# Turning attention tiles on TensorE instead of by transposing transfers, in a fused attention and ELU layer kernel

## The chip, the cores and the metric

The kernel runs on one core of one Trainium2 chip. A core has five engines with a queue each: TensorE (PE, with PEld for its weight loads), VectorE (DVE), ScalarE (ACT), GpSimd (POOL) and SyncE (SP), and 16 DMA engines. The metric is the time on the device in microseconds.

## The reference, cut to what matters

```python
# q, k, v: [8, 8, 576, 64] (batch, head, position, depth)
scores = scale * np.matmul(q, k.transpose(0, 1, 3, 2))
bias = slopes[:, None, None] * (-np.abs(rel).astype(np.float32))[None, :, :]
mask = (rel >= 0) & (rel < window)                      # window = 128
scores = np.where(mask, scores + bias[None], -1000000000.0)
scores = scores - np.max(scores, axis=-1, keepdims=True)
attn = np.exp(scores)
attn = attn / (np.sum(attn, axis=-1, keepdims=True) + 1e-09)
attn_out = np.matmul(attn, v)
x = attn_out.transpose(0, 2, 1, 3).reshape(B * S, H * D)        # [4608, 512]
h = x @ w_in                                                    # [4608, 2048]
g = np.where(h > 0.0, h, alpha * (np.exp(np.minimum(h, 0.0)) - 1.0))
out = g @ w_out                                                 # [4608, 512]
```

A causal attention with a sliding window of 128 positions and a linear bias by distance, and behind it two dense layers with an ELU between them.

## The kernel before

**Attention.** Each batch of 576 positions is cut into key blocks of 128 (`u`). `scores` (L215) computes four groups of heads at once, each on 32 rows of the array, into four PSUM banks `sp[0]` to `sp[3]`. The first two banks are one tile, `spa`, the other two are the tiles `sp2` and `sp3`. `expo` (L227) takes the exponential on ScalarE: one instruction over both banks of `spa` (L230), and one each for `sp2` and `sp3` (L233). `weigh` (L236) multiplies by the table of the bias and the mask on VectorE. `all_values` (L263, matmuls at L271) multiplies by V for 128 query positions at a time, with a column of ones in V that gives the sum; `rden` is its reciprocal (L277), and L279 writes the normalised tile `xn` (positions by 512 features). The fifth tile of a batch has 64 positions and goes through `values` (L240) in two parts. The first two batches have loads and scores of their own (`turn_first`, `first_scores` and so on).

**Turning.** The dense layer needs the features on the partitions, so each `xn` is turned into a ring `xT` that holds three batches. Nine tiles, those of batch 0 and the first four of batch 1, are turned by TensorE: `turn_x` (L289) issues four transposes against the identity (L295) into a PSUM bank, and ScalarE or VectorE copies the result to `xT` (L297). The other 31 tiles go through `turn` (L283): one transposing transfer on SP's queue (L287), from `xn` to `xT`.

**Dense layers.** `hidden` (L304) computes a piece of x @ w_in in a PSUM bank, mostly `hp[0]` and `hp[1]` in turn, eight matmuls of 256 columns at L312. ScalarE makes the exponential of the negative part of it: a relu and an exponential (L319, L321) where the step is in the set `SOFT`, or one exponential (L323) with a clamp on GpSimd (L325). `elu` (L329) forms g on VectorE (L333). The second layer, from block 1 on, works on blocks of 256 tokens, 18 in all, each by seven products of half size (`product`, L397, matmuls at L403) instead of eight, with sums on VectorE (`sums`, `combine`, `lower`, through `add`, L364), copies on ScalarE (`keep`, L410 and L412) and stores on SP's queue (`put`, L434). Its banks are `op` and `av`, for block 1 also `sp[3]`.

**What sets the order.** All work of the main part is called by a long string of letters, `SCRIPT` (L539): each letter takes the next call from its own list, and so fixes the order in every engine's queue. `h` is the matmuls of `hidden`, `p` and `q` its two steps behind them, `e` the elu, `o` one matmul of a product (`o5` five of them), `k` the scores, `x`, `y`, `z` the exponentials, `w` the weighting, `v`, `r`, `n` the values, their reciprocal and their normalising, `T` a transposing transfer, `t` the transposes of `turn_x` and `tA` or `tD` its copy, `d` VectorE's turning of q and k, `s1` to `s4`, `c1` to `c4`, `u` and `m` the rest of a product block, `l` a load, `P`, `U` and `Z` the last block. An engine works its queue in order and waits at an instruction whose inputs or whose bank are not free.

Of the kernel before, what the change touches and what calls it, by code (L numbers as in the profile page):

```python
# [7 lines left out]
F32 = mybir.dt.float32  # L8
F16 = mybir.dt.float16
# [9 lines left out]
def kernel(  # L19
# [57 lines left out]
    sp = [spa[:, 0, :], spa[:, 1, :]] + [ps_s.tile([128, 512], F32, name=f"sp{i}", tag=f"sp{i}") for i in (2, 3)]  # L77
# [72 lines left out]
    with tc.manual_schedule():  # L150
# [76 lines left out]
        def expo(b, u, g):  # L227
            if g < 2:
                if g == 0:
                    nc.scalar.activation(unit(b, u)[:, 0:2, :, :], spa.rearrange("p g (h c) -> p g h c", h=2),  # L230
                                         AF.Exp, scale=0.125)
                return
            nc.scalar.activation(unit(b, u)[:, g, :, :], sp[g].rearrange("p (h c) -> p h c", h=2),  # L233
                                 AF.Exp, scale=0.125)
# [48 lines left out]
        def turn(b, i):  # L283
            n = 128 if i < 4 else 64
            o = (b * S + 128 * i) % RING
            x = xnt.pop((b, i)).rearrange("p g h d -> p (g h d)")
            nc.sync.dma_start_transpose(out=xT[:, :, o:o + n], in_=x[0:n, :])  # L287

        def turn_x(b, i, copy, bank):  # L289
            n = 128 if i < 4 else 64  # L290
            o = (b * S + 128 * i) % RING
            x = xnt.pop((b, i)).rearrange("p g h d -> p (g h d)")
            t = bank.bitcast(F16)[:, 0:512].rearrange("p (c r) -> p c r", c=4)
            for c in range(4):
                nc.tensor.transpose(t[:, c, 0:n], x[0:n, 128 * c:128 * c + 128], ident[0:n, 0:n])  # L295
            yield
            copy(xT[:, :, o:o + n], t[:, :, 0:n])  # L297
# [222 lines left out]
        for b in range(2, B):  # L520
# [19 lines left out]
            f fD f fD b f fA f fD C C C C b i j i j j b i j j v r n v r n b t tD v r n v r n  # L540
            h p q t tD f fA
            e h p q i j f fD f fA f fD b b i j i l
            h p q e j j l
            h p q e b i l
            h p q j v r n v r n e l
            h p q t tD b i j e l
            h p q e
            h p q e
            h p q e v r n v r n
            h p q e l O  # L550
            h p q e v r n t tA l
            h p q e a v r n l l l O
            h p q e a t tA
            h p q e a l O
            h p q e a l O O1 O2
            h p q e a l O
            h p q e a f fD f fA l l O
            h p q e a f fA f fD f fA f fA l l O
            e a l l s1 s3 O O1 O2 i j i j j
            W l l o7  # L560
            s2 W l l o1 u o6 v r n i j i j j
            l l o2 c1 o5 v r n
            W W d l o3 u o4 t tA i j v r n
            W l s4 o4 u o3 v r n
            h p q v r n i j d l
            h p q e W t tA d l o5 u o2
            h p q e v r n i j l
            h p q e W t tA l o7 c2
            h p q e v r n i j d l
            h p q e W l o7 u  # L570
            h p q e v r n v r n l c3 m s1
            o1 h o2 p o1 k l q o1 e o1 v y l t tA d o1
            h x r n e o1 T o1 p o4 s2 u
            h q w o2 e o2 z o4 d p o1
            h w q c1 o2 p v e o4 q o1 r
            h s3 u n o2 p o2 e o1 T o1 u k s4 q o1
            h x e d o2 p o3
            h w u q y l o1 z e o4 p o2 d o1
            h d q w l o1 e v p o2 c2 l o1 q o1
            h r n l o1 e o1 T p o2 l o2 s1 o1 q k l u o1 e o1 x  # L580
            h l d o2 p o1 s2 o4 u
            h w q y e o4 z o2 c3 o2 p o2 w m
            h q c1 v u e p o4 s3 o1 q o1
            h r n o2 p o1 e o1 T o1 k q s4 u
            h e x d o3 p o2 w o1
            h y q z l o1 e o1 u o3 p o1 w o2
            h q d l o1 v c2 p e o1 l o2 q o2 r o2 v l u e v o2
            h r l s1 n o2 p o2
            h r T n q n o2 p e k u d o1 q o3
            h x s2 e o2 p o3 w o3 q o1  # L590
            h c1 y e o1 z o2 s3 o2 p o3 w o1
            h u q c3 v m e T o3 u o2 r o1 p s4 o3
            h n q o1 e T o1 p k d u q
            h x l e o2 p o1 w o4 z o1 q
            h c2 y l e o2 p o2 w l o4 q
            h s1 l e o1 v l p o2 r o1 q l
            h n u d o2 p k e q o3 s2 o2 u
            h x e s3 o2 p o3
            h w q c1 y o1 e o4 z o2 c3 o2 p o1 s4
            h m T u w q o4 e v u p o2 r o3 n o1 q o1  # L600
            h T e o3 u k p c3 q
            h x l e o2 p o2 w o3 y o1 q
            h c2 z l e o2 p o2 w l o2
            h q s1 l v e p l o2 r o1 u v d q o1 m l o1
            h e o1 n o1 p o4 v r T q s2 o3
            h u e o1 s3 o1 p o2
            h r n q c1 o2 n p o3 e o1 T o2 q k d u
            h x e s4 o2 p o1
            h w z d q o5 u o2 e o1 p o4 y o2 q o1
            h u w o1 e o1 p o3 v c3  # L610
            h q r n l o2 e p o1 T o2 l o2 s3 q k l u c2
            h x e m l o3 p
            h w l q s1 l o2 z o2 e o3 y o5 p o1 w
            h q s2 v u e p o4 c1 o1 q
            h r n o2 e p o1 T o4 u s4 k q
            h x e d o2 p o3
            h w u q o1 y o1 e o4 p o2 d o1
            h z q u w l o2 p o3 e o2 v q
            h l r e o1 l n o1 p o5 s3 l T q k c2 u l e
            h x l o2 p o1 w o1  # L620
            h l q s1 o1 z o1 e o4 y o2 c3 o2 p
            h w m q s2 o1 v u p o1 v r o1 e o2 q o1 v c1 o3 e o1
            h u n o2 r p o1 T o1 n
            h r q n o2 T p e o3 k u s4 q
            h x e o2 d o1 p o4
            h z w q y e o2 u o2 p o2 w o4 q
            h c2 l e o2 p v l o2 r o2 s1 q o1
            h l u n o1 l o1 e p o1 T o2 k d l q o1
            h x e o2 p o1 w
            h u s2 q o3 z o1 e o4 y o2 c3 o1  # L630
            h p w m q c1 o1 v e o4 u o2 r o1 p
            h n q s3 T k p e o2 q o1 d o3
            h x e o1 s4 u o3 p
            h w z q o3 l u o1 e o2 p o4 y o1 c2 o1 q o1
            h w l v e p l o2 r o2 c3 o1 l o1 u
            h n q l s1 T m o2 p k e l q s3 o1
            h l x e l o1 s2 o1 p o5 d u o2 q o1
            h z e o1 y o2 w o2 p o2
            h w q c1 o2 e p v v q r o2 s4 o1
            h u e o2 n p v o3 r o1 q T o1 n o3 r o1 u o1 n o1  # L640
            h u e T d o1 k p o1 q x
            h e o2 p o1 w o4 y
            h q c2 z l e o2 p o3 w l o3 q
            h s1 l e o2 p v l o2 r o1 u
            h s2 q l n o2 p o2 c3 o3 u e o1 m T q k d
            h x e o2 p o1 w o1
            h q c1 o1 z o1 e o4 y o2 s3 o2 p
            h w q o2 v u e p o3 s4 o1 u o2
            h q r n o2 p o1 e o1 T o1 k q d
            h x e o2 u o1 w o1 p o5 y o1 q o3 z  # L650
            h e c3 o2 p
            h c2 w q o3 p v e u o2 r o1 q o1 m o1 n
            h s1 T o1 k p e u d q o3
            h x s2 e o2 p o4 c1 o1 z o2 s3 o1
            h q y e o3 p o2 w o2 u o2
            h q w e o2 p v s4 o1 u o1 v q r o2 r v
            h e n o2 p o2 r o1 T n o1
            h n q T e k p o1 u o1 q o1 x o3
            h c2 e o2 s3 p o4
            h y s1 q w o2 p o3 e o2 z o2 c3  # L660
            h u w q m o1 e v p o4 s2 u o2 q
            h r n o2 p o1 e o1 T o2 k q c1
            h x e o2 p o1 w o1
            h u q o2 z o1 e o4 p o2 s4 o2 y o1
            h q w o1 u o1 v e p o2 r o1 q u
            h n e T o2 p o2 k q o1 x o2
            h c2 e y o3 s1 p
            h q s2 o4 e o2 u o3 z o1 w o2
            h p w q o4 u o1 e v p o2 r o1 q o1
            h n s4 o1 k p e q c1 o3 c3  # L670
            h x e m T o1 s3 o1 p o3
            h w u q o1 z o1 e o4 y o4 p o1
            h w q o1 v u e p v o3 q o1 u o1
            h e o1 r o1 p o1 r o1 n o1
            h q c2 T v e p o6 s1 q o2
            h u r e o2 n p o3 c3 o1
            h q s2 e o2 p o4 n o1 u o1
            h s3 q T m e o2 p o3 c1 o2
            h q e o2 p o5
            h q u e o2 p o3 s4 o2  # L680
            h q u e o2 p o5
# [166 lines left out]
```

## Time and profile before

| | |
|---|---|
| time, median of 3 runs | 304.71 us (304.34 to 305.03) |
| the profiled execution: its time, its span | 304.94 us, 303.2 us |
| TensorE, weight loads | 296.2 us (98%), 255.6 us (84%) |
| VectorE, ScalarE, GpSimd | 256.2, 238.2, 109.1 us |
| transposing transfers `xT<-xn` | 31, median 3.1 us from issue to landing |
| nine tiles turned by TensorE | 36 matmuls at L295; copies on ScalarE 0.58 us (64 rows: 0.35) |

The span runs from the first to the last instruction of the profiled execution. "Busy" is the time in which an engine has an instruction under way. Matmuls overlap in the array, so a matmul's own duration is longer than its share of TensorE's time: that is read from the distance between starts. A chain is followed back from the last instruction, at each step to what released it.

### The profile page before, as it was taken

The page shows a single profiled execution, that of the slowest core. Times are in us where ns is not written, and L with a number is a line of the kernel's source. Part 1 is how long each engine was busy: PE and PEld are TensorE (multiplying, and loading weights), DVE is VectorE, ACT ScalarE, POOL GpSimd, SP SyncE. Part 2 cuts the span into 40 slices and gives each one's busy share as a digit, 9 for nine tenths or more (in the row PEclk, how much of TensorE's full clock was granted, in tenths as well). Part 3 has the DMA queues.
Part 4 walks back from the last instruction along what each step waited for, and adds up shares of the span by engine and source line. Part 5 has one row for each costly group of instructions (what it writes and reads, how often), then busy time and mean ns, then how long its engine had stood idle before and what let it go on. Part 6 is the DMA issues. An engine that isn't in the chain of part 4 may idle for free.

```text
span 303.2 us, 9837 instructions
## 1 busy us (share of the span) xinstructions
PE 296.2 (98%) x4074; PEld 255.6 (84%) x4074; DVE 256.2 (85%) x499; ACT 238.2 (79%) x445; POOL 109.1 (36%) x163
## 2 busy tenths in 40 slices
PE   7899999999999999999999999999999999999996
PEld 5688876989888889988888888887899888898885
DVE  5747879989999999799989898989989887885873
ACT  5577688869797888877979888888887888868881
POOL 8947958671534243332534162606000100010000
PEclk9999999999999999999999999999999999999999
DMA  8999999999394949491969695999220301111013
GB/s 99 193 198 201 201 178 192 125 128 101 36 160 72 131 78 119 83 184 21 161 60 130 107 118 66 130 144 125 61 89 2 97 17 54 54 56 43 37 57 118
DMA packets 96941, 32.04 MB, mean 106 GB/s; under 512 B 83968, under 2 KB 92800, under 8 KB 96896
## 3 DMA queue, kind: packets, MB, share of 16 engines
q0 software_dynamic: 75920, 18.36, 66.6%
q1 hardware_dynamic: 20832, 12.98, 18.0%
q8 instruction: 32, 0.52, 0.7%
q14 instruction: 13, 0.11, 0.1%
q10 hardware_dynamic: 144, 0.07, 0.1%
HBM read 36.70 MB, written 9.44 MB: 152 GB/s over the span
## 4 chain that ended last, share of the span: by engine, by line
PE 86%; DVE 4%; DMA 4%; ACT 2%; POOL 2%; issue 1%; POOLq 0%; DVEq 0%; ACTq 0%
PE hp L312 38%; PE op L403 15%; PE av L403 14%; PE spa L222 4%; PE spa L271 3%; DMA VP<-in_v_dram 2%; PE sp L403 2%; PE sp L312 2%; DMA xT<-xn 2%; PE sp L250 1%; DVE g L333 1%; PE op L339 1%; PE spa L339 1%; ACT e L323 1%; DVE xn L259 1%
## 5 line engine op out<-in xcount | busy, mean ns | idle before, releaser
L312 PE MATMUL hp<-xT,wi 128*128 128x256 f16 (+3 forms) x1488 | 144.1, 245 | 0.9 <-DMA xT<-xn 0.4
L312 PEld LDWEIGHTS <-wi 128*128 128x128 f16 x1600 | 120.6, 98 | 15.1 <-issue 3.9
L333 DVE SCALAR_TENSOR_TENSOR g<-e,hp 128x512 f16<-128x512 f32 x138 | 93.9, 681 | 23.4 <-ACT e L321 12.0
L325 POOL TENSOR_SCALAR e<-e 128x512 f32<-128x512 f32 x44 | 28.9, 657 | 151.4 <-ACT e L323 148.6
L319 ACT ACTIVATE e<-hp 128x512 f32<-128x512 f32 x98 | 58.7, 599 | 28.2 <-PE hp L312 22.9
L321 ACT ACTIVATE e<-e 128x512 f32<-128x512 f32 x100 | 63.6, 636 | 2.2
L403 PEld LDWEIGHTS <-S 128*128 128x128 f16 x544 | 51.0, 98 | 6.6 <-issue 1.1
L403 PEld LDWEIGHTS <-g 128*128 128x128 f16 x400 | 37.1, 98 | 5.4 <-issue 1.5
L238 DVE TENSOR_TENSOR EX<-EX,TAB 128x1024 f16<-128x1024 f16 x48 | 33.0, 694 | 2.8 <-ACT EX L233 1.3
L114 POOL DMA_DIRECT2D VP<-in_v_dram x40 | 34.4, 874 | 1.7 <-DMA s<-in_k_dram 1.3
L323 ACT ACTIVATE e<-hp 128x512 f32<-128x512 f32 x40 | 24.2, 605 | 12.1 <-PE hp L312 12.0
L403 PE MATMUL op<-T,S 128*128 128x256 f16 x192 | 29.5, 273 | 0.0
L403 PE MATMUL av<-T,S 128*128 128x256 f16 x176 | 27.0, 273 | 0.0
L233 ACT ACTIVATE EX<-sp 128x512 f16<-128x512 f32 x48 | 27.0, 602 | 0.0
L230 ACT ACTIVATE EX<-spa 128x1024 f16<-128x1024 f32 x24 | 24.5, 1022 | 1.0 <-PE spa L222 0.5
L364 DVE TENSOR_TENSOR S<-g 128x1024 f16<-128x1024 f16 (+2 forms) x35 | 23.1, 666 | 0.3 <-PE op L403 0.2
L403 PE MATMUL op<-wo,g 128*128 128x256 f16 x128 | 20.4, 273 | 0.0
L403 PE MATMUL av<-wo,g 128*128 128x256 f16 x120 | 19.7, 273 | 0.0
L108 POOL DMA_DIRECT2D st<-in_k_dram x24 | 16.3, 687 | 2.9 <-DMA s<-in_q_dram 2.0
L279 DVE TENSOR_TENSOR xn<-spa,rden 128x512 f16<-128x512 f32 x24 | 16.5, 687 | 0.4
L108 POOL DMA_DIRECT2D st<-in_q_dram x24 | 15.9, 666 | 1.3 <-DMA VP<-in_v_dram 1.3
L222 PE MATMUL spa<-QT,KT 32*128 32x256 f16 (+2 forms) x240 | 15.1, 250 | 0.0
(137 smaller groups left out, 381.5 us busy)
## 6 DMA issues: line engine op xcount, KB each, us to landing
out_dram<-ob SPq DMA_DIRECT2D x32, 256.0 KB, 3.2
VP<-in_v_dram POOLq DMA_DIRECT2D x32, 128.0 KB, 6.1
st<-in_k_dram POOLq DMA_DIRECT2D x24, 144.0 KB, 5.3
st<-in_q_dram POOLq DMA_DIRECT2D x24, 144.0 KB, 5.9
wi<-in_moe_w_in_dram POOLq DMA_DIRECT2D x4, 512.0 KB, 11.2
wo<-in_moe_w_out_dram POOLq DMA_DIRECT2D x4, 512.0 KB, 10.8
out_dram<-ob SPq DMA_DIRECT2D x7, 128.0 KB, 1.7
VP<-in_v_dram POOLq DMA_DIRECT2D x8, 64.0 KB, 6.1
```

Of the source, the lines that this page charges most:

```text
L108: nc.gpsimd.dma_start(st[b][32 * g:32 * g + 32, w, :, :, :, :].rearrange("p h n j d -> p (h n) (j d)"), (q, k)[w][b, 2 * g:2 * g + 2, :, : ...
L114: nc.gpsimd.dma_start(VP[b % 2][0:p, n, :, 0:D], v[b, :, 128 * n:128 * n + p, :].rearrange("h p d -> p h d"))
L222: nc.tensor.matmul(sp[g][:, 256 * h2 + o:256 * h2 + o + n], kt_[b % 2][r, k0:k0 + 255:2], qt_[b % 2][r, c0:c0 + 2 * n - 1:2], start=dh == ...
L233: nc.scalar.activation(unit(b, u)[:, g, :, :], sp[g].rearrange("p (h c) -> p h c", h=2), AF.Exp, scale=0.125)
L238: V.tensor_tensor(out=e, in0=e, in1=TAB[:, int(u == 3), 2 * gp:2 * gp + 2, :, :], op=ALU.mult)
L312: nc.tensor.matmul(p[:, l * w + u0:l * w + u1], w_in_sb[:, c, fc * 128:(fc + 1) * 128], xT[:, c, x0:x0 + u1 - u0], start=(c == 0), stop=(c ...
L319: nc.scalar.activation(e[:, 0:n], p[:, 0:n], AF.Relu, scale=-1.0)
L321: nc.scalar.activation(e[:, 0:n], e[:, 0:n], AF.Exp, scale=-1.0)
L323: nc.scalar.activation(e[:, 0:n], p[:, 0:n], AF.Exp)
L325: nc.gpsimd.tensor_scalar(out=e[:, 0:n], in0=e[:, 0:n], scalar1=1.0, scalar2=0.0, op0=ALU.min, op1=ALU.max)
L333: V.scalar_tensor_tensor(out=gs[t][:, f0:f0 + nf, c0:c0 + w], in0=sh(es.pop((t, c0, f0))), scalar=1.0, in1=sh(hps.pop((t, c0, f0))), op0=A ...
L403: nc.tensor.matmul(o, a[:, j, :], b[:, j, :], start=j == 0 and i in (1, 2, 5), stop=j == 7, skip_group_check=True)
```

## The change

`sp2` and `sp3` become one tile of two banks, `spb`, as `spa` is already, and `expo` takes one exponential over both banks of it. `turn` and its transfers are gone: all 31 tiles go through `turn_x` with the bank `sp[3]`, which is the second half of `spb`, and with ScalarE's copy. The letters `z` and `T` go, 31 times `t` and `tA` come, and the script is written anew around them.

```diff
     spa = ps_s.tile([128, 2, 512], F32, name="spa", tag="spa")
-    sp = [spa[:, 0, :], spa[:, 1, :]] + [ps_s.tile([128, 512], F32, name=f"sp{i}", tag=f"sp{i}") for i in (2, 3)]
+    spb = ps_s.tile([128, 2, 512], F32, name="spb", tag="spb")
+    sp = [t[:, i, :] for t in (spa, spb) for i in range(2)]
...
         def expo(b, u, g):
-            if g < 2:
-                if g == 0:
-                    nc.scalar.activation(unit(b, u)[:, 0:2, :, :], spa.rearrange("p g (h c) -> p g h c", h=2),
-                                         AF.Exp, scale=0.125)
-                return
-            nc.scalar.activation(unit(b, u)[:, g, :, :], sp[g].rearrange("p (h c) -> p h c", h=2),
+            nc.scalar.activation(unit(b, u)[:, g:g + 2, :, :], (spa, spb)[g // 2].rearrange("p g (h c) -> p g h c", h=2),
                                  AF.Exp, scale=0.125)
...
-        def turn(b, i):
-            n = 128 if i < 4 else 64
-            o = (b * S + 128 * i) % RING
-            x = xnt.pop((b, i)).rearrange("p g h d -> p (g h d)")
-            nc.sync.dma_start_transpose(out=xT[:, :, o:o + n], in_=x[0:n, :])
-
-        def turn_x(b, i, copy, bank):
+        def turn_x(b, i, copy, bank, c0=0):
...
-            t = bank.bitcast(F16)[:, 0:512].rearrange("p (c r) -> p c r", c=4)
+            t = bank.bitcast(F16)[:, c0:c0 + 512].rearrange("p (c r) -> p c r", c=4)
...
         for b, i in [(1, 4)] + [(b, i) for b in range(2, B) for i in range(5)]:
-            job("T", turn, b, i)
+            parts(turn_x(b, i, copies[0], sp[3]), "t", "tA")
...
-                for g, x in ((0, "x"), (2, "y"), (3, "z")):
+                for g, x in ((0, "x"), (2, "y")):
```

Of the script, one batch's stretch, before and after:

```diff
-            h q s2 v u e p o4 c1 o1 q
-            h r n o2 e p o1 T o4 u s4 k q
-            h x e d o2 p o3
-            h w u q o1 y o1 e o4 p o2 d o1
-            h z q u w l o2 p o3 e o2 v q
+            h c1 q s4 o2 y o1 e o6 c3 o2 p
+            h w m q w t u o2 e o1 tA v p o2 r o1
+            h n q d u o2 t o1 e o1 tA o5 p o1 k u q c3
+            h x l e s3 o2 p
+            h w y q o3 l o1 e o2 p o4 w l o1
```

The end of the script changes too: one of the last block's products (`P`) and several single ones (`o`) now stand before or between the last steps of `hidden` and `elu`.

More of the change, by code (lines that the diff above doesn't have):

```diff
@@ L539 @@
         SCRIPT = """
[L540 to L576, printed above, removed]
-            h x e d o2 p o3
-            h w u q y l o1 z e o4 p o2 d o1
-            h d q w l o1 e v p o2 c2 l o1 q o1
-            h r n l o1 e o1 T p o2 l o2 s1 o1 q k l u o1 e o1 x
@@ L581 @@
[L581 to L613, printed above, removed]
-            h q s2 v u e p o4 c1 o1 q
-            h r n o2 e p o1 T o4 u s4 k q
-            h x e d o2 p o3
-            h w u q o1 y o1 e o4 p o2 d o1
@@ L618 @@
-            h z q u w l o2 p o3 e o2 v q
[L619 to L681, printed above, removed]
-            h q u e o2 p o5
-            h q e o2 p o3 c2 o2
-            h s1 q u e o2 p o3 s3 o2
-            h q e o2 p o3 s2 o2
-            h q u e o2 p o3 s4 o2
-            h q c1 e o2 p o3 c3 o2
-            h q m u e o2 p o5 q u
-            h p q e s3 o5 u o2
-            h p q e s1 s2 o7 c2
-            e s1 s2 P U o7 u
-            c4 P c1 s4 P U P U
-            P U P c4 c2 Z
+            f f fD b fD f f fA b fD i C C C i j b C i j v v b r j n r j n t j tD v v r
@@ new lines @@
+            h n r n p t f tD q fA
+            h e f i fD f j f fA fD b p b i q i j
+            h l e
+            h p q b p
+            h l e j j q v i p r l n v
+            h j r q n e t l p b e i q tD
+            h j l v p
+            h r e q v p
+            h e q n
+            h r p e q v n p O e q
+            h r a l e
+            h p a q t O n tA l e p v
+            h l q l O e p r l n q
+            h a l e t p
+            h a l q
+            h p e l O a l p tA O l q q l e
+            h a l f e p l f s3 q l
@@ new lines @@
+            h fA e l O fD p l O q l s1 O1 f s2 l O2 f fA e f l f fD O fA fA l i O1 a o3 l j o1 a O2 o2 i l o1 j o1 W i j o5 u o1 W o1 j v o1 i r c1 o2 j o1 n o1 v o1 j i r n o3 W o2 u t o1 W o1 tA o1 v o2 j d o3 r
+            h s4 W v p i n
+            h u r q j n d l o2 e o2 p o1 v W o2 q t
+            h r tA l n e o2 p i d v u q
+            h j r n l e o1 t p o2 d o1
+            h tA q W l e o1 i p v d j
+            h q c2 r l e o2 p o2 n o2
+            h W q l e v p o1 v r o1
+            h r q u n s1 l o2 p t n o1 l o1 e o1 tA v o1 q k r l n s2 o1 x o3
@@ new lines @@
+            h e y s3 o2
+            h w p w u o3 q o5 p o1 e o1 t o1 q
+            h tA e v c1 p o1
+            h r u n q o1 d o2 p o1 t e o2 tA o3 c3 o2 q o1 s4 m k e
+            h x o1 u o2 w o1 p
+            h d u q y o2 d o1 l o2 e o2 p o4 w o2 q
+            h c2 l e o1 v p d l
+            h r q n l o2 c3 p o1 t l s1 o2 tA o4 e l q k u
+            h e l x m s2 o2 p o2 w
+            h u s3 q o2 p o1 e o4 y o2 c1 o2
+            h q w o2 p o1 v e u o2 q r o1
+            h n d t o2 tA o1 e o3 p k d q o1 s4 o1
@@ new lines @@
+            h x e o2 d p
+            h u q w y o3 l o1 e o3 p o2 w o1
+            h u q d l v p c2 v r l o2 e q o5 l o1 e
+            h l r n v p o1
+            h r n u n q o1 s1 o2 p o1 t e o2 tA o4 c3 u k q s2 m o1
+            h x e s4 o2 p o3 w o3 q o2 c1 o1
+            h y e o1 s3 o2 p o2
+            h w u q o2 p e t v o1 q o1 r o1
+            h n u tA e o2 p t o1 d o2 tA o1 q o3 u o1 k l e
+            h x o2 p o1 w o3
+            h y q c2 l e o2 p o4 w o2 l q o2
+            h s1 u l e v p l o2 r o1
@@ new lines @@
+            h q n l s2 o2 p k e q o5 x
+            h e s3 u o2 p o1
+            h c1 q s4 o2 y o1 e o6 c3 o2 p
[3 more added lines that the diff above has]
+            h w y q o3 l o1 e o2 p o4 w l o1
+            h q c2 l e v p l o1 s1 o1 v q
+            h l s2 u m o1 e o1 p o4 r o2 n u o1
+            h q r e v p o3 r o2 n
+            h q n d t o2 c1 tA o3 e o2 p t o1 d o1 tA o1 u k q d
+            h x e o2 s4 p o3
@@ new lines @@
+            h w q y o1 e o8 p
+            h w u q o1 v p o1 e o3 u o1 q o1 r o1
+            h n l c2 o2 c3 p t l o1 e o2 tA o3 q k l u
+            h e x m l o2 p
+            h w l q s1 l o3 p o1 e o4 y o2 s2 o4
+            h q w u v e p o2 r o1
+            h q n c1 o2 e p t o3 tA o1 s3 o3 u k s4 q
+            h x d e o2 p o3 d o2 u o1
+            h q w y o1 e o6 p o1 w o3 u o1 v q o1 l
+            h e r c2
+            h p n q o1 t p o2 l o1 e o1 tA o3 k c3 u l q s3 m l
+            h x e l o2 p o1 w
@@ new lines @@
+            h l q s1 l o2 y o1 e o8 p
+            h w q s2 o1 v u e p v o2 r o1 q o1 c1 o1 v r
+            h r e o1 n o1 p o4
+            h n q n u e o1 t o2 tA o1 d o4 p t
+            h tA q o1 u o1 e p k s4 o1 q x
+            h e o1 y o2 w o6 p o1
+            h c2 u q w o2 p l v e o4 q r
+            h l n s1 o2 l p t o1 e o2 tA o1 k l s2 q d u
+            h x l e o2 p o1 w o1
+            h u s3 q o2 p o1 e o4 y o3 c1
+            h q w o3 p o1 v e o2 r o2 c3 u
+            h q n m o1 e o1 p t o2 d o1 tA o4 q k u e
@@ new lines @@
+            h x d
+            h p s4 y q o1 w o4 l o2 e o1 u o2 p o5 c2 o1 q o1
+            h w l e o1 v p l
+            h r q l n o1 s1 l p t o2 tA o1 e o1 l o1 k q s2 l e o1 x
+            h l o1 u o1 w o1 p o4 s3 o1 u o2 q o4 c1 o1 y o1
+            h e s4 o2 p o3 w
+            h q c3 u v m e p v r o2 q r o2 n o1 v o2 r
+            h n n e o2 p o2 t o1 u o2 tA
+            h q t e o2 tA o1 p k d u q
+            h x e o2 p o4
+            h y q c2 c3 l o1 e o1 p o4 w o2 l q o2
+            h w u l m e v p o3 r o1 s1 l o2 q o2
@@ new lines @@
+            h n u l e o2 p o1 t d o1
+            h tA s2 q k p e o1 x o2 s4 o3
+            h c1 q w y o3 e o5 p
+            h w q s3 o3 u v e p o2 r o2 q
+            h n u e t o2 d tA o5 p k u q
+            h x e o2 p o1 w o4 y o1 q o1
+            h e o2 p o1 c2 o2
+            h w q u o1 e o1 p v o2 q r
+            h n s3 o1 t o2 tA s1 o4 p k e u s2 q o3
+            h x e d o2 p o4 c1 o2 q
+            h w y e o4 s4 o2 p
+            h w q o1 c3 o1 p o1 v e m u v q r o1 v r o1 n o1 u
+            h r n n o2 p o2 e o2 t q o2 tA o1
@@ new lines @@
+            h e t o2 tA o1 p k u q
+            h x e o2 p o2 c2 o3 s1 o1 q o1
+            h y e o3 w o2 p
+            h w q o3 u o1 e v p o3 r o1
+            h q n u s2 t p o3 e o2 tA o3 s3 o1 q k e
+            h x c1 o2 p o1 w o4 u o1 s4
+            h q y e o7 p o1 w
+            h q c3 v m u e p o4 r o1 u
+            h q n e t o2 tA o5 p k c2 q
+            h x e o2 p o2 s1 o4 q o1 w o3
+            h u e y s2 o3
+            h p w q o4 u o1 e o1 p o2 v q
+            h r n o2 e p o2 k c3 q c1 m o1 x
@@ new lines @@
+            h e o1 y
+            h w s4 p o4 s3 o1 u t q o2 w o3 p o3 e o2 u o2 q v
+            h tA r e o1 v p v o2 u o1 q o1
+            h e o2 p r o2 n
+            h q r c2 o2 e p o6 n q o2
+            h n e o2 s3 p o2
+            h u s1 q o2 p o1 e o3 t q o1 s2 o2
+            h u e tA o1 s4 o1 p o2 t c1 o2 tA
+            h q e o2 p o4 c3 o1
+            h q m u e o2 p o4
+            h q u e o2 p o6 q s3
+            h u e o2 p o4
+            h q e o2 p o4 c2 o2 q
+            h s1 u e o2 p o2 s2 o2
@@ L694 @@
+            h q e o2 p o6 q
+            h u e o2 p o2 s4 o3
+            h q c1 e o2 p o5
+            h q u e o2 p o3 c3 o2
+            h q m u e o2 p o5 s3 o1 q
+            h u e o2 p o3 s1 o1 P q c2 s2 o2 U o1 e o4 P u s1 s2 c4 P c1 s4 P U P U P U c4 c2 Z
         """
```

## The prediction

> **What bounds the kernel now.** I read the page's first two parts, then the chain that ended last, then the waits of TensorE alone, then busy time by stretch, and last the timeline of TensorE around the places that the change touches.
>
> ```profile
> PE 296.2 (98%) x4074; PEld 255.6 (84%) x4074; DVE 256.2 (85%) x499; ACT 238.2 (79%) x445; POOL 109.1 (36%) x163
> ...
> PE   7899999999999999999999999999999999999996
> ...
> PEclk9999999999999999999999999999999999999999
> ```
>
> TensorE is busy in nearly every slice, at the full granted clock; VectorE and ScalarE are not full. A busy PE need not be a fast one, so the pace has to be read too. Start times in the timeline of TensorE (columns: start, duration, what, count) give it:
>
> ```profile
> 102.66 1.04 PE L312 MATMUL hp<-xT,wi 128*128 128x256 f16 x8
> 103.53 0.49 PE L403 MATMUL av<-wo,g 128*128 128x256 f16 x3
> 103.86 0.82 PE L403 MATMUL op<-T,S 128*128 128x256 f16 x6
> 104.51 1.04 PE L312 MATMUL hp<-xT,wi 128*128 128x256 f16 x8
> ```
>
> Eight matmuls of 256 columns start 0.87 us before what follows, so 0.109 us each; nine of L403 take 103.53 to 104.51, again 0.109 each. The groups follow each other with no hole. This is the stream itself, not a queue waiting inside a busy bar. The chain that ended last, by engine, says the same:
>
> ```profile
> PE 86%; DVE 4%; DMA 4%; ACT 2%; POOL 2%; issue 1%; POOLq 0%; DVEq 0%; ACTq 0%
> ```
>
> Of the waits of TensorE, longest in total first (columns: us, times, longest), one concerns the transposing transfers:
>
> ```profile
> PE hp L312 <- DMA xT<-xn: 0.4, 1, 0.4
> ```
>
> And busy time in one long stretch (its length, then PE, PEld, DVE, ACT, POOL):
>
> ```profile
> 60.00:293.00 233.00, 232.38 (x3032) 203.50 (x3030) 205.30 (x385) 192.77 (x366) 65.15 (x93) 1.00 0.71 89
> ```
>
> TensorE lacks only 233.00 - 232.38 = 0.62 us here, and 0.4 us of that is the only wait for a transposing transfer in the whole run. All 31 of these transfers lie in this stretch (issued from 70.0 to 272.2 us), and so will what replaces them. The chain's 2% for "DMA xT<-xn" is one 4.68 us transfer at 200.4 us; the chain walks through its whole duration, but TensorE worked beside it and lost only that wait.
>
> **The change, part by part.**
>
> *The transposes on TensorE.* 31 tiles x 4 = 124 matmuls are added; nothing else on TensorE changes in number. The kernel already turns nine tiles this way (L295), so their price is in the trace:
>
> ```profile
> 60.44 0.39 PE L295 MATMUL av<-ident,xn 128*128 128x128 f16 x4
> 60.66 0.49 PE L403 MATMUL op<-wo,S 128*128 128x256 f16 x3
> ...
> 34.13 0.67 PE L312 MATMUL hp<-xT,wi 128*128 128x128 f16 x9
> 34.73 0.29 PE L295 MATMUL sp<-ident,xn 64*128 64x64 f16 x4
> 34.95 0.56 PE L312 MATMUL sp<-xT,wi 128*128 128x128 f16 x7
> ```
>
> A full tile's four take 60.66 - 60.44 = 0.22 us. A tile of 64 rows (the fifth of a batch) takes 34.95 - 34.73 = 0.22 us, and the nine matmuls before it take 0.60 us where nine of 128 columns at 0.056 are 0.50, so 0.10 us goes to the change of tile shape: 0.32 us in all. Six batches with four full tiles are 24 x 0.22 = 5.3 us, seven short tiles (batch 1's and those of the six) are 7 x 0.32 = 2.2 us. Sum **7.5 us**, on the engine that has 0.62 us of holes there. It goes on the path in full.
>
> Here a rule of the Trainium skill is to be weighed. "VectorE: DVE Perf Modes", section "The three transpose paths", gives 390 ns for a 128x128 transpose on TensorE against 1309 ns on the DMA crossbar, and its rules for kernel authors advise TensorE wherever a PSUM destination is acceptable. Read as speed, it promises a gain: this trace too has a transfer landing 3.1 us after issue at the median, against about a microsecond for four transposes and a copy. But it compares latencies, and a tile's latency cost this kernel 0.4 us once. What counts is the time that TensorE is occupied. Its 390 ns taken as occupancy would be an estimate of 124 x 0.39 = 48 us (353 us in all); the row's 0.22 us for four, in a stream, makes it 7.5. I take the row.
>
> *The transfers that go.* SP's queue loses 31 issues of about 1.2 us each (median 1196 ns), which stood between the stores of the output. Nothing on the path waits for those stores, so I put the relief at nothing; it would count only if the output buffers came free late, and no engine is seen waiting for them. POOL's queue of loads keeps its transfers. Their landing may come sooner; no wait for them stands in 60 to 293 us on TensorE. What is surely saved is the wait at 205.24 us, whose matmul starts 0.67 us after one that needs 0.11: **-0.56 us**.
>
> *The copies and the exponentials on ScalarE.*
>
> ```profile
> L233 ACT ACTIVATE EX<-sp 128x512 f16<-128x512 f32 x48 | 27.0, 602 | 0.0
> L230 ACT ACTIVATE EX<-spa 128x1024 f16<-128x1024 f32 x24 | 24.5, 1022 | 1.0 <-PE spa L222 0.5 <-PE sp L222 0.4
> L297 ACT COPY xT<-av 128x512 f16<-128x512 f16 x3 | 1.7, 582 | 0.1
> L297 ACT COPY xT<-sp 128x256 f16<-128x256 f16 x1 | 0.4, 353 | 0.0
> ```
>
> Added: 24 x 0.58 + 7 x 0.35 = 16.4 us. Saved: 24 units, each 2 x 0.602 - 1.022 = 0.18, so 4.4 us. ScalarE goes from 238 to about 250 us, and in the stretch from 192.8 of 233 to 204.8 of about 240, 83% to 85%. It doesn't become the bound. Its own saving is worth nothing on the path.
>
> *New waits.* Three are added to TensorE's queue, and everything behind the waiting instruction (the next 8 of L312 and the products of L403) waits with it, and then L319/L323 and L333 behind that. (a) The transposes wait for xn: after the last matmul of the weighted values VectorE needs 0.20 (L277) + 0.69 (L279), and the last matmul's own 0.19. The new order usually leaves one L312 group and five products between, 0.87 + 5 x 0.109 = 1.42 us, against 1.08 plus whatever VectorE has in front; one more L333 at 0.68 is already too much. (b) The next scores write the bank that the copy has to empty: often two products (0.22) before the copy's place and three to five (0.33 to 0.55) after it, about 0.55 to 0.77 us against 0.58 plus ScalarE's backlog. (c) L312 reads xT after the copy; one to two microseconds are left, ample. Also the copy pushes the chain L319, L321, L333, which frees hp for the L312 after next, by 0.58, while the transposes delay that L312 by 0.22. From below these waits cost 0, where the order fits; from above, a full 0.58 - 0.22 = 0.36 at each of the 31 tiles plus the odd wait for xn, 11 us. The nearest row is the order before, just as tight between L333 and L312: TensorE idles 0.62 us in all there. I take **+1.3 us**, nearer the low end.
>
> *Beginning and end.* The script is rewritten from its first letter, but up to the first hidden group TensorE does the same work behind the same loads (the chain starts with V's 7.42 us transfer), and the last products are only pulled ahead of the last L333. In 0 to 60 us PE is busy 56.44, 3.56 idle, most of it before the first tiles are loaded. I take 0, between -1 and +1.
>
> *Sum*, against the profiled execution: span 303.2, its time 304.94, so 1.7 lies around the span. 304.94 + 7.5 - 0.56 + 1.3 = 313.2. The median of the runs is 0.23 below the profiled one: **313.0 us**, a ratio of 1.027.
>
> **The rivals.**
> - *Waits take over* (VectorE or ScalarE late for the transposes and for the scores behind them). For it: DVE at 205 of 233 us, and margins of tenths. Against: the added TensorE time relieves VectorE, whose work is unchanged, to about 85%. If half of the 31 tiles meet one VectorE instruction of 0.68 us with nothing to spare, 16 x 0.4 = 6 us more: 315 to 321, say 318.
> - *The transposes hide in TensorE's holes.* For it: small gaps at each change to the scores' 32-row tiles (24 units). Against: those come with the change of shape and remain, and idle time is 0.62 us. If a new order closed other gaps as well, 309 to 311.
> - *Faster.* One mechanism: the rewritten order packs the first 60 us better, where TensorE idles 3.56 us behind loads and changes its tile shape most often (0.10 us each time, as above). It decides when more than 7.5 us is recovered there; the idle time isn't that much, so forty changes of shape would have to go as well, while the first L312, at 12.8 us, keeps its place behind the same loads. It would give some 303.5.
> - *No change*: the added matmuls run beside something that ends later. For it only the 2% of the chain on the transfers. 304.7.
>
> **How the numbers follow.** My own case, 311 to 315: 0.63. Waits, over 315: 0.19. Partly hidden, up to 311: 0.13. No change 0.02, faster 0.03. Leaving out half of the waits' upper part and the lowest cases, the range is 310.0 to 317.5. Within 0.2% (0.6 us) is about what a measurement of this kernel can't tell from no change. Slower 0.95, same 0.02, faster 0.03.
>
> **What would show it.** Right: TensorE's count up by 124 to about 4198 and its busy time by about 7 us; the transposes' groups in the timeline still 0.22 us apart from what follows; ScalarE near 250 us; TensorE's idle time in the long stretch at 1 to 2 us. The waits' rival: waits of L295 for VectorE's xn, or of L222 for ScalarE's xT, several us in sum. Wrong altogether: the transposes costing clearly more than 0.22 us in the stream (then 316 and up), or a stretch between 20 and 60 us that gets shorter by microseconds.

## The result, and the profile after

The changed kernel takes 319.86 us (median of 4 runs, 319.16 to 320.16) against 304.65 us: 1.0495 times as long, 95% interval 1.0474 to 1.0517, or 15.1 us more. The forecast was 313.0 with a range up to 317.5. It had the sign, and 8.3 of the 15.1 us. The profiled execution took 319.16 us, its span is 317.4. Single runs of one kernel below differ by up to 1% with the granted clock (twice the transposes: 324.3 and 324.5 us at 1.0, 326.8 and 326.9 us at 0.994 and 0.992), so parts of one or two microseconds are read from the traces, whose mean clock is 0.998 to 1.0.

Page after: busy times, TensorE by slices, the chain by engine.

```profile
PE 307.0 (97%) x4198; PEld 262.3 (83%) x4198; DVE 257.7 (81%) x499; ACT 250.1 (79%) x452; POOL 109.9 (35%) x163
...
PE   7889999989999999999999999999999999999995
...
PE 85%; DVE 5%; ACT 4%; issue 2%; DMA 2%; POOL 1%; DVEq 0%; POOLq 0%; ACTq 0%
```

TensorE has its 124 matmuls more (4074 to 4198) and is 10.8 us busier. ScalarE came out at 250.1, as worked out. The other 3.4 us of the span are idle time of TensorE. Three of its waits, and its busy time in the long stretch (which ends 12 us later now):

```profile
PE spb L393 <- DVE xn L255: 1.0, 2, 0.5
PE hp L302 <- DVE g L323: 0.9, 3, 0.5
...
PE spb L223 <- ACT xT L287: 0.3, 1, 0.3
```

```profile
60.00:305.00 245.00, 242.70 (x3171) 210.58 (x3169) 208.01 (x387) 204.80 (x373) 66.56 (x94) 1.00 0.53 70
```

Idle went from 0.62 to 245.00 - 242.70 = 2.3 us. The first and the third row are waits at the new tile `spb`. Before, no row was a wait for a reader of these two banks (the one row at `sp`, 0.2 us, waits for an input, the weighted scores). The transposes themselves (L285) stand in the stream as the forecast had them:

```profile
113.34 0.38 PE L393 MATMUL op<-T,S 128*128 128x256 f16 x2
113.56 0.39 PE L285 MATMUL spb<-ident,xn 128*128 128x128 f16 x4
113.78 0.71 PE L393 MATMUL op<-T,S 128*128 128x256 f16 x5
```

They start 0.22 us before what follows, with no hole ahead of them. Over all 31 groups these distances, with the 0.1 us by which a group of 64 rows starts late, sum to 7.5 us, the forecast's figure. So the excess lies elsewhere, and two more places show where to look. The first is a scores unit, the matmuls of one call of `scores` (rows of two matmuls: start, duration). Before:

```profile
101.64 0.29 PE L222 MATMUL spa<-QT,KT 32*128 32x256 f16 x2
101.65 0.29 PE L222 MATMUL sp<-QT,KT 32*128 32x256 f16 x2
...
102.00 0.28 PE L222 MATMUL sp<-QT,KT 32*128 32x256 f16 x2
102.21 0.39 PE L403 MATMUL av<-wo,g 128*128 128x256 f16 x2
```

After, with ScalarE's copy of the tile turned just before:

```profile
105.53 0.59 ACT L287 COPY xT<-spb 128x512 f16<-128x512 f16 x1
106.08 0.29 PE L223 MATMUL spa<-QT,KT 32*128 32x256 f16 x2
106.16 0.29 PE L223 MATMUL spb<-QT,KT 32*128 32x256 f16 x2
...
106.51 0.28 PE L223 MATMUL spb<-QT,KT 32*128 32x256 f16 x2
106.72 0.28 PE L393 MATMUL av<-wo,g 128*128 128x256 f16 x1
```

The four groups of heads used to start within 0.01 us of each other. Now the pair on `spb` starts 0.08 us late, when the copy out of the bank has ended (105.53 + 0.59), and stays behind to the end of the unit: 0.64 us in place of 0.57. Over all 24 units, from the first start to that of the next other matmul, it is 15.80 us against 13.63. PE counts as busy all through it. This is the price of the copy and hardly of the tile: in the experiments below the units take 15.21 us with two tiles, and 13.72 with two tiles and no copies. The tile makes the first unit alone longer (1.14 against 0.65 us).

The second is the longest kind of wait. TensorE, then VectorE, after:

```profile
65.38 0.60 PE L393 MATMUL spb<-T,g 128*128 128x256 f16 x4
66.50 0.38 PE L393 MATMUL spb<-T,g 128*128 128x256 f16 x2 [0.52 <-DVE xn L255]
```

```profile
66.02 0.43 DVE L255 TENSOR_TENSOR xn<-spb,rden 128x256 f16<-128x256 f32 x1 [0.23 <-PE spb L393]
```

These products accumulate in the fourth bank (`sp[3]`); L255 reads values out of the third. There is nothing to wait for, except that both are now one tile. L255 itself had waited 0.23 us for the first four of these products. Call this a crossed wait: one bank's work waits for the other bank's.

### The profile page after: what moved, and what is told of

It is laid out like the page before. It is cut to its first block, busy times and chain, and to the rows that moved or that the text cites. A ratio compares the mean times of both kernels' runs of the same rounds, so it can differ in the third digit from the quotient of the medians.

```text
span 317.4 us, 9996 instructions
## 1 busy us (share of the span) xinstructions
PE 307.0 (97%) x4198; PEld 262.3 (83%) x4198; DVE 257.7 (81%) x499; ACT 250.1 (79%) x452; POOL 109.9 (35%) x163
## 4 chain that ended last, share of the span: by engine, by line
PE 85%; DVE 5%; ACT 4%; issue 2%; DMA 2%; POOL 1%; DVEq 0%; POOLq 0%; ACTq 0%
PE hp L302 36%; PE op L393 14%; PE av L393 13%; PE spa L267 3%; PE spa L223 3%; PE spb L285 2%; PE spb L393 2%; PE spb L223 2%; DMA s<-in_q_dram 2%; PE spb L302 1%; DVE g L323 1%; PE spb L246 1%; PE op L329 1%; PE spa L329 1%; DVE xn L255 1%
## 5 line engine op out<-in xcount | busy, mean ns | idle before, releaser
L393 PEld LDWEIGHTS <-S 128*128 128x128 f16 x544 | 50.3, 98 | 6.3 <-issue 0.9
L234 DVE TENSOR_TENSOR EX<-EX,TAB 128x1024 f16<-128x1024 f16 x48 | 33.7, 708 | 4.7 <-ACT EX L229 4.1
L393 PE MATMUL op<-T,S 128*128 128x256 f16 x192 | 30.7, 273 | 0.0
L393 PE MATMUL av<-T,S 128*128 128x256 f16 x176 | 28.1, 273 | 0.0
L229 ACT ACTIVATE EX<-spb 128x1024 f16<-128x1024 f32 x24 | 24.5, 1020 | 0.0
L287 ACT COPY xT<-spb 128x512 f16<-128x512 f16 (+1 forms) x34 | 18.2, 536 | 6.8 <-PE spb L285 6.5
L393 PE MATMUL av<-wo,g 128*128 128x256 f16 x120 | 18.7, 273 | 0.0
```

Of the source, the lines that this page charges most:

```text
L229: nc.scalar.activation(unit(b, u)[:, g:g + 2, :, :], (spa, spb)[g // 2].rearrange("p g (h c) -> p g h c", h=2), AF.Exp, scale=0.125)
L234: V.tensor_tensor(out=e, in0=e, in1=TAB[:, int(u == 3), 2 * gp:2 * gp + 2, :, :], op=ALU.mult)
L393: nc.tensor.matmul(o, a[:, j, :], b[:, j, :], start=j == 0 and i in (1, 2, 5), stop=j == 7, skip_group_check=True)
```

## The experiments

Each run is compared by its ratio to the runs of before made along with it; differences in microseconds are differences of these ratios times 304.7.

**The merged tile alone.** Order and transfers of before, one exponential over both banks.

```diff
+    spb = ps_s.tile([128, 2, 512], F32, name="spb", tag="spb")
+    sp = [t[:, i, :] for t in (spa, spb) for i in range(2)]
...
-                for g, x in ((0, "x"), (2, "y"), (3, "z")):
+                for g, x in ((0, "x"), (2, "y")):
```

> The kernel before with one part of the change alone: the last two score banks as one tile with one exponential, and the order of before without the letter z. The 31 tiles still go by transposing transfers. Theory one (the loss comes from the turning on TensorE, about 7 us, and from waits that its bank, its copies and the new order bring): 304 to 305 us, no difference. Rival (the merged tile itself holds up scores and exponentials): 306 us or more.

Measured 315.55 us, ratio 1.0334 (1.0291 to 1.0377): 10.2 us more, with not one transpose added. Theory one fell here. The part that I had costed as a small saving on ScalarE costs, in the order of before, as much as two thirds of the whole loss.

**Only the declaration.** To tell the tile from the exponential:

```diff
-    sp = [spa[:, 0, :], spa[:, 1, :]] + [ps_s.tile([128, 512], F32, name=f"sp{i}", tag=f"sp{i}") for i in (2, 3)]
+    spb = ps_s.tile([128, 2, 512], F32, name="spb", tag="spb")
+    sp = [t[:, i, :] for t in (spa, spb) for i in range(2)]
```

> The kernel before with two lines changed: the third and fourth score banks are declared as one tile of two banks. Exponentials (two, one a bank), transfers and order stay as before. Theory two (the declaration makes accesses to one bank wait for readers of the other): about as much as with the one exponential, 315 us. Rival (the one exponential, which needs both banks and frees both late, is the cost): 304.7.

312.93 us, ratio 1.028 (1.0242 to 1.0317): 8.5 us from two lines that change no operand and no bank, only the semaphores. TensorE's waits in this run:

```profile
PE spb L313 <- ACT xT L298: 1.4, 1, 1.4
PE spb L137 <- ACT KT L142: 1.3, 1, 1.3
...
PE spb L251 <- DVE g L334: 1.0, 1, 1.0
PE spb L251 <- ACT U L411: 0.7, 1, 0.7
PE spb L404 <- DVE xn L260: 0.6, 1, 0.6
PE spb L404 <- DVE ob L365: 0.6, 1, 0.6
```

In the first row `hidden` wants to write the third bank and waits until ScalarE has copied a turned tile out of the fourth; in the others the banks are crossed in the same way. In the order of before such pairs stand close together, because they were free of each other. In the built program the two banks lie where they lay before, and some thirty matmuls into them wait for other or later readers than they did.

All of these rows but the last start before 78.5 us, the last behind 299. Between the two the list has one row:

```profile
PE hp L313 <- DVE EX L239: 0.3, 1, 0.3
```

So the tile's cost lies in the first part, where `hidden`, the values, the turns of the first two batches and the products of block 1 share these two banks: from the first matmul of `hidden` to the 501st (70.9 us before) it takes 64.9 us in place of 58.1, and from there to the last 221.8 in place of 221.5. The one exponential adds some 1.7 us to it (10.2 - 8.5; the intervals overlap, so this part isn't sure).

**The turning alone.** Two tiles and the order of before, each transfer replaced by the transposes and the copy, where the bank was free.

```diff
-            job("T", turn, b, i)
+            parts(turn_x(b, i, copies[0], sp[3]), "T", "tT")
...
-            h r n o2 e p o1 T o4 u s4 k q
+            h r n o2 e p o1 T tT o4 u s4 k q
```

> The kernel before with the other part of the change alone: the 31 tiles turned by TensorE into the fourth score bank and copied by ScalarE, the third and fourth banks still two tiles with two exponentials, and the order of before. Each turn stands where its transfer stood, or, at seven places where the bank still holds scores or values, right behind their last reader; the copy follows at once. Theory two (the merged tile ties its two banks together: a write to one waits for a reader of the other; the turning itself costs TensorE's 7.1 us and some waits for xn and for the bank): 304.7 + 7.1 + 3 = 314.8 us. Rival (the turning needs the new order, the waits for it are the main loss): 320 or more.

327.5 us, ratio 1.0743 (1.0725 to 1.0761): worse than the whole change, as the rival said. Its waits, the longest at these banks:

```profile
PE sp L222 <- ACT xT L297: 4.5, 14, 0.5
PE sp L295 <- ACT xT L297: 1.4, 3, 0.7
...
PE sp L295 <- ACT EX L233: 0.9, 2, 0.6
PE sp L250 <- ACT xT L297: 0.7, 1, 0.7
```

The scores wait for the copy, and their units take 23.3 us in sum in place of 13.6. The old order left no room between a turn and the next scores; so the turning does need another order.

**The new order, with and without the turns and the tile.** Four kernels with the new order: the merged tile with no turns, and with transposes but no copies; then the same pair with two tiles; and the changed kernel with two tiles. Without turns:

```diff
+        def LATER(b, i):
+            xnt.pop((b, i))
+            yield
+            yield
...
-            parts(turn_x(b, i, copies[0], sp[3]), "t", "tA")
+            parts(LATER(b, i), "t", "tA")
```

Without copies alone, `LATER` runs `turn_x` to its first yield. Two tiles: the declaration and `expo` of before, with `z` right behind each `y`. Kernels without turns or copies also have one memset of a part of `xT` on GpSimd.

> The changed kernel with the 31 turns left out altogether, transposes and copies both; xT keeps zeros and old columns there, so the output isn't the reference's. New order and merged tile stay. Theory one: 319.9 - 7.1 (transposes) - 2.2 (scores' units stretched by the bank) - some 2.5 (copies in ScalarE's queue) = 308 us, 3 us above before, from the rewritten beginning and end. Rival A (everything beyond the transposes is the new order's): 312.7. Rival B (everything beyond them is the copies'): 305.

> The changed kernel with the 31 groups of four transposes, but without their copies to xT (which keeps zeros and old columns there, so the output isn't the reference's). Theory one: 319.9 - 2.2 - 2.5 = 315.2 us. Rival A (the new order's waits): 319.9. Rival B (the copies are all of the rest): 312.

> The changed kernel with the third and fourth banks as two tiles again, each with its own exponential (the second right behind the first); new order and turning stay. Theory two: the waits across the two banks go, 0.68 twice, 0.23, 0.3 and half of the 2.2 us by which the scores' units are stretched: 319.9 - 3.0 = 316.9 us. Rival (the new order and the turning are the whole loss, the tile nothing): 319.9.

> As the kernel with the two tiles again and the new order, but with the 31 turns left out, transposes and copies (xT keeps zeros and old columns there, so the output isn't the reference's): the new order alone. Theory two: 312.2 - 1.9 = 310.3 us, of which 5.6 above before would be the new order's own. If the order costs nothing by itself: 305. If the tile costs nothing in it: 312.2.

> New order, two tiles, the 31 groups of transposes without their copies to xT (zeros and old columns stand there, so the output isn't the reference's): lies between the kernel without turns (309.2) and the one with them (316.7). If the transposes are on the path in full, 309.2 + 7.1 = 316.3, and the copies cost 0.4. If a part runs in holes of the new order, as in the merged pair (317.1 - 312.2 = 4.9), 314.1, and the copies cost 2.6 through the bank that they hold and ScalarE's queue.

| new order | no turns | transposes | transposes and copies |
|---|---|---|---|
| two tiles | 309.23, 1.0149 (1.0127 to 1.0172) | 316.25, 1.0381 (1.0347 to 1.0415) | 316.73, 1.0387 (1.0371 to 1.0403) |
| one tile | 312.21, 1.0234 (1.0173 to 1.0295) | 317.14, 1.0394 (1.0357 to 1.0431) | 319.86, 1.0495 (1.0474 to 1.0517) |

Read along the upper row: new order alone +4.5 us, transposes +7.1, copies +0.2. Down the last column: the tile +3.3. In the lower row the transposes come to 4.9 and the copies to 3.1. But these intervals are 0.5 to 1.9 us wide on either side, too wide for the copies. The traces are finer. From the first matmul of `hidden` to the last (rows of `hp`: shortest, median and longest duration in ns, then first and last start), before and after:

```profile
L312 PE MATMUL hp<-xT,wi x1488: 193/271/283, 12.8 to 292.4; 128*128 128x256 f16 x96, 128*128 128x128 f16 x62, 128*128 128x192 f16 x16, 128*128 128x64 f16 x12
L302 PE MATMUL hp<-xT,wi x1488: 189/270/283, 12.4 to 305.6; 128*128 128x256 f16 x96, 128*128 128x128 f16 x62, 128*128 128x192 f16 x16, 128*128 128x64 f16 x12
```

With two decimals this distance is 279.59 us before, and in the new order:

| first to last matmul of `hidden` | no turns | transposes | transposes and copies |
|---|---|---|---|
| two tiles | 282.37 | 288.23 | 290.28 |
| one tile | 284.99 | 290.64 | 293.22 |

Now the rows agree: order +2.8, transposes +5.9 and +5.7, copies +2.1 and +2.6, the tile +2.6, +2.4 and +2.9. Of the tile's 2.9 in the changed kernel, 2.6 lie ahead of the 501st of these matmuls (73.3 us), in the first part again; in the long stretch behind, one tile costs 0.3 with the copies and nothing without. The copies' 2.1 are mostly the scores' units, 15.21 us in place of 13.72. The transposes occupy 7.5 us of the stream and lengthen it by 5.9: the waits of `hidden` behind a product, measured as further below, fall at the same time from 3.6 to 2.1 us, so a part of the added work fills holes of the new order. Outside this distance the start varies with the loads (12.4 to 14.6 us up to the first of these matmuls), and 1.0 us is added behind the last one.

Two tiles take the crossed waits away; this is what is left in TensorE's list, with new order and turns, apart from the start:

```profile
PE hp L306 <- DVE g L327: 1.1, 4, 0.5
```

**Twice the transposes**, in the changed kernel:

```diff
+            f = turn_x(b, i, copies[0], sp[3])
+            next(f)
+            xnt[b, i] = x
+            g = turn_x(b, i, copies[0], sp[3])
+            next(g)
```

> The changed kernel with each of the 31 groups of four transposes issued twice, into the same columns, before the one copy. If a group is on the path in full, 31 x 0.22 us, with 0.22 for the short ones too since the second group changes no tile shape: 24 x 0.22 + 7 x 0.12 = 6.1 us more, 326.0 us. If TensorE's waits take up a part of it (the second group runs while something else is waited for): 322 to 324.

325.66 us, ratio 1.0692 (1.0644 to 1.0739): 6.0 us more than the changed kernel, near the 6.1 worked out. The traces say it more closely: the second groups occupy 6.2 us of the stream, and the distance from the first to the last matmul of `hidden` grows by 5.1 (298.32 against 293.22). So most of each group is paid, and about 1 us falls into waits that were there anyway.

**The upper half of the bank.**

```diff
-            parts(turn_x(b, i, copies[0], sp[3]), "t", "tA")
+            parts(turn_x(b, i, copies[0], sp[3], 512), "t", "tA")
```

> The changed kernel with the transposes in the upper half of the fourth score bank (columns of the second pair of heads, which the next scores write last) in place of the lower half. Theory one, in which the scores wait for the copy to leave the bank (24 units take 15.8 us in place of 13.6): most of 2.2 us comes back, 318.0 us, and the scores' units are near 0.57 us each again. If the bank isn't what stretches the scores: 319.9, units unchanged.

319.54 us, ratio 1.0491 (1.0442 to 1.0541), units 15.8 us as before this edit. The scores don't wait for columns, so a free half of the bank is of no use. Whether they wait for the bank or for the tile this run can't tell.

**Copies on VectorE**, `copies[1]` in place of `copies[0]`:

> The changed kernel with the 31 copies on VectorE in place of ScalarE (0.42 against 0.58 us). If ScalarE's queue is what the copies cost, by the exponentials behind them: 318. If VectorE, busy for 86% in the long stretch, is the tighter one: 321 to 323, with more waits of L302 for the elu.

321.48 us, ratio 1.0555 (1.0532 to 1.0578), 1.8 us worse. The expected sign, more waits for the elu, isn't there (0.8 us in all); the scores wait longer for the copy, with units of 18.5 us in place of 15.8. VectorE is the later of the two.

**Where the new order loses.** The order of before with the new beginning, and with the new end; and the new order (two tiles, no turns) with the old end. Both orders have made the same calls at the cut near the end, and nearly the same at the 28th group of L312; the few that differ were put behind the cut. The edit at the end, with the unchanged first letters left out:

```diff
-            h q m u e o2 p o5 q u
-            h p q e s3 o5 u o2
-            h p q e s1 s2 o7 c2
-            e s1 s2 P U o7 u
-            c4 P c1 s4 P U P U
-            P U P c4 c2 Z
+            h q m u e o2 p o5 s3 o1 q
+            h u e o2 p o3 s1 o1 P q c2 s2 o2 U o1 e o4 P u s1 s2 c4 P c1 s4 P U P U P U c4 c2 Z
```

> The kernel before (two tiles, transposing transfers) with the new order up to the 28th group of L312, some 70 us, and the order of before from there on. The new order alone, two tiles and no turns, came to 309.2, 4.5 above before; its trace puts the loss behind 62 us and at the very end. If so: 304.7 to 305.3. If the rewritten beginning carries it: 307 or more.

305.46 us, ratio 1.0013 (0.9992 to 1.0033): no difference.

> The kernel before with the new order for its last four groups of L312 and all behind them alone; up to there both orders have done the same calls. The profiles of the new order end 3.9 to 4.3 us after the last matmul of TensorE starts, where before ends 3.0. If the rewritten end is that part of the new order's 4.5 us: 305.5 to 305.9. If the late end is due to what stands in front: 304.7.

305.0 us, ratio 0.9997 (0.9976 to 1.0018): no difference.

> The new order with two tiles and without the turns (xT keeps zeros and old columns there, so the output isn't the reference's), with the order of before for the last four groups of L312 and all behind. With the new end it took 309.2. If the end is worth 1 us: 308.2, and the middle's waits of L302 for the elu are left as the main part. If the end is worth nothing: 309.2.

310.13 us, ratio 1.0184 (1.0147 to 1.022), no better than with the new end. So neither the rewritten beginning nor the rewritten end carries the 4.5 us. In the traces 2.8 us of it lie between the first and the last matmul of `hidden`, in the middle, and 1.1 behind the last one (11.86 us against 10.75). That last part is there with the old end too (11.69), and not where the new end follows the order of before (10.65); what makes it stays open. Busy time there (length; PE first), the kernel before and then the new order alone:

```profile
66.00:290.00 224.00, 223.38 (x2873) 195.08 (x2869) 198.19 (x372) 185.79 (x353) 60.70 (x86) 1.00 0.71 88
```

```profile
66.00:293.00 227.00, 225.26 (x2884) 195.57 (x2882) 197.76 (x371) 187.52 (x354) 61.43 (x87) 1.00 0.54 71
```

Idle is 1.74 us against 0.62, and of the 3 us more, 1.2 are eleven matmuls more (x2884). An instance, on TensorE and VectorE:

```profile
176.49 0.60 PE L399 MATMUL op<-T,g 128*128 128x256 f16 x4
177.54 0.92 PE L308 MATMUL hp<-xT,wi 128*128 128x256 f16 x7 [0.45 <-DVE g L329]
```

```profile
176.80 0.69 DVE L329 SCALAR_TENSOR_TENSOR g<-e,hp 128x512 f16<-128x512 f32 x1 [0.51 <-POOL e L321]
```

`hidden` wants its bank before the elu two groups back has read it, and that elu waits for GpSimd's clamp. Waits of this kind (distance of the starts less the pace, a product ahead of an L308) sum to 3.6 us in the new order alone and 1.7 in before. This names some two fifths of the 4.5 us, or two thirds of the middle's 2.8. Which lines of the script would have to move wasn't tried, and it stays open.

## Why the prediction was wrong, point by point

- **TensorE bounds the kernel, at full pace.** Right. It explains why every wait of a few tenths shows in the time.
- **The transposes, 7.5 us, in full on the path.** The price was right: they occupy 7.5 us of the stream. "In full" was not quite: they lengthen it by 5.9 us, because a part falls into waits that the new order brought. The row of this trace was the right price; the 390 ns of the Trainium skill ("VectorE: DVE Perf Modes", "The three transpose paths") taken as occupancy would be wrong by a factor of seven here. That page's advice to prefer TensorE where a PSUM destination is acceptable was a loss all the same, because a tile's latency was not what the kernel waited for.
- **The transfers that go, -0.56 us.** The wait went with them, but it was no fixed cost: the two kernels with the order of before in the middle and a new beginning or end keep the transfers, and their traces don't have it either.
- **"It doesn't become the bound. Its own saving is worth nothing on the path."** True of ScalarE's time, and the first step that failed. I took the merged tile for an exponential and priced its instructions at nothing. It was also a statement about which accesses are ordered: 3.3 us in the new order (2.9 in the traces), 8.5 us in the old one. With two tiles the kernel takes 316.7 us, inside the range; the tile takes it out. I counted waits on the bank of the copies (b), but never asked what a write to the third bank would wait for.
- **New waits, +1.3 us, from "the order before" as the nearest row.** The second step that failed. That order wasn't a row for the new one: the new order costs 4.5 us before a single tile is turned, 2.8 of them in the middle. The copies add 2.1, mostly through margin (b): the scores wait for the bank. So the two make 4.9 us in the middle where I took 1.3. Margins (a) and (c) hold: on the long stretch no wait for xn is listed, nor one for a copy into xT.
- **Beginning and end at 0.** Right for the new order with two tiles. In the changed kernel the beginning fails: from the first to the 501st matmul of `hidden` it takes 60.9 us in place of 58.1, and 2.6 of these 2.9 us are the tile's. The end comes 1.0 us later behind the last of these matmuls, unexplained as said.
- **The rivals.** "Waits take over", 318 us at 0.19, came nearest in size. One of its waits is real, ScalarE's copy late for the scores, some 1.5 us; VectorE late for the transposes was not seen, and it too left the tile out.

The sum as measured, by the times: 304.7 + 4.5 (order) + 7.1 (transposes) + 0.2 (copies) + 3.3 (tile) = 319.8 us. By the traces, first to last matmul of `hidden`: 279.59 + 2.78 + 5.86 + 2.05 + 2.94 = 293.22 us. No version with the turns on TensorE came near the kernel before, and none is to be expected that adds 7.5 us of work to an engine without holes.

## What to carry to other kernels

When two buffers become one tile, list every pair of accesses that used one each and stand close together: they may now wait for each other, whatever columns they touch, and no instruction in the diff shows it. A hand-made order is tuned to the waits of one set of tiles; move work or tiles and it has to be priced anew, and a run of the order alone, with the moved work left out, separates the two. On an engine without holes, price added work by the distance of starts in its stream. And where times scatter by a microsecond, the distance between two fixed instructions in the traces can separate what the medians can't.

## What the runs showed that I had not expected

One group of heads that starts late sets the end of a whole scores unit: a pair 0.08 us late made a unit of 0.57 us one of 0.64, though each wait is far below what an idle row reports. And a busy TensorE hid it: of 2.2 us of stretched units 0.3 us stand in the list of waits.
